# Eight weight operations ahead of the first half-step, and earlier operand loads, in a two-layer expert on one core

## The chip, the cores and the metric

The kernel runs on one core of a Trainium2 chip. The metric is the device time of one launch in microseconds. Three runs of the kernel before stand beside one profiled execution, from which all rows below come.

## The reference

Three stages follow each other. Attention (32 heads, queries averaged in pairs, 1152 keys) gives 2304 tokens of 512 values. A dense expert with an inner width of 2048 follows: this is the stage of the change. Then eight routed experts, of which each token whose skip score is above 0 takes one.

```python
def _moe_ref(x, w_in, w_out):
    h = x @ w_in                                  # 2304 x 512 by 512 x 2048
    g = h * (1.0 / (1.0 + np.exp(-1.702 * h)))
    return (g @ w_out).astype(np.float32)         # 2304 x 2048 by 2048 x 512
```

The setup multiplies the float32 weights `w_in` and `w_out` by a double-precision scalar, so both come as 64-bit floats. Only float32 accuracy is wanted at the end.

## The kernel before, in words

**Two-part operands.** TensorE multiplies in a float32 format of reduced precision (`F32R`). Each operand is therefore split into a high half and a low half, and a product takes three matmuls: high by high, high by low, low by high.

**Weights of the dense expert.** There are 16 blocks (`fb`) of 128 inner columns. A block has two units: unit 2fb is its 128 columns of `w_in` (gives `wih` and `wil`), unit 2fb+1 its 128 rows of `w_out` (`woh` and `wol`). `wload` (L423) fetches a unit of 512 KB through SP's queue into one of three `wr` buffers; `wsplit` (L432) takes the 64-bit floats apart with integer operations. A unit has seven VectorE operations on 128 x 512 elements, `v[0]` to `v[6]` (L453 to L459), and three ScalarE operations: the absolute value of the upper words (L461, needed by `v[1]`), a scaled conversion (L462, after `v[2]`, needed by `v[6]`) and the high half itself (L463, after `v[4]`). `v[6]` writes the low half. Units 0 to 3 are split during attention, units 4 to 31 (blocks 2 to 15) in the first pass of `ffn`: 28 x 7 = 196 VectorE operations.

**Order of the split.** The generator `blocks()` in `ffn` hands these operations out one at a time. `v[5]` and `v[6]` of a unit are put among the first operations of the next unit: unit u+1 yields `v[0]`, then `v[5]` of unit u, `v[1]`, `v[2]`, `v[3]`, then `v[6]` of unit u, then its own `v[4]`. `make(u)` runs between `v[3]` and `v[4]` of unit u-1; it issues the load of unit u+2 and the absolute value of unit u. The other two ScalarE operations are appended to the list `after`, and run when `act()` is called next (or earlier, where `need()` finds that the following operation depends on one). `fill(k)` takes k entries, first from the queue `fq` (routing work, empty in the first pass), then from `blocks()`.

**Passes and half-steps.** Tokens go through in six passes of `CH` = 768, 384, 256, 256, 256, 384 tokens. A pass is cut into pieces of at most 384 tokens, so the first has two, the others one. For each block and piece the loop at the end of `ffn` runs one half-step g: `layer1` of this half-step, then `layer2` of the half-step two before (`LAG`), then `rstep` and the entries of the agenda `ag` that are due. `layer1` makes 12 matmuls into one of two PSUM buffers `h` (L599), the sigmoid on ScalarE (L604), the multiplication on VectorE (L605, the last reader of `h`), the high half `gh` on ScalarE (L606), `act()`, `fill(fa)`, the low half `gl` on VectorE (L609) and `fill(fb_)`. `layer2` makes 9 matmuls of 512 columns (L624 to L626). Each engine works through its instructions in this written order. In the first pass fa and fb_ are 3 and 3 for piece 0, 3 and 4 for piece 1.

**Operands of the next pass.** `xload` (L466) fetches `X` and the reciprocals `RD`, repeated over 64 partitions, into the single buffer `xraw` through SP's queue; `xnorm` (L474, its instruction L476) multiplies them into one of four `xa` buffers, on VectorE for the second pass; `xsplit` makes `xh` (L485, ScalarE) and `xl` (L489, VectorE). For the second pass there are four of each (j = 0 to 3). The operand tiles of piece 0 of the first pass are the ones that `xsplit` overwrites, so it is due in half-step 30, after layer 1 of that half-step has read them. In half-step numbers `first[0, 12]` is 24: loads are due at 23 + 2j, products at 24 + 2j. Agenda entries that are due at the same half-step run in the order in which they were put in: j, then load, product, split.

**Before the first half-step.** Attention ends with the `dn` matmuls (L326), whose result ScalarE copies into `dr` (L327) and sends off as `DEN` with two DMA issues (L331). Then `constants()` puts a few GpSimd operations and a `memset` of VectorE (L523) in line, and half-step 0 follows.

Of the kernel before, what the change touches and what calls it, by code (L numbers as in the profile page):

```python
# [39 lines left out]
def pieces(n):  # L40
    k = -(-n // 384)
    return [(i * (n // k), n // k) for i in range(k)]
# [29 lines left out]
class Kernel:  # L72
# [5 lines left out]
    def dma(self, out, in_):  # L78
        if out.dtype == F32R:
            out = out.bitcast(F32)  # L80
        if in_.dtype == F32R:
            in_ = in_.bitcast(F32)
        self.nc.sync.dma_start(out, in_)
# [407 lines left out]
    def ffn(self, ctx):  # L491
# [22 lines left out]
        def constants():  # L514
            nc.gpsimd.memset(ONE, 1.0)
            nc.gpsimd.memset(U, 1.0)
            nc.gpsimd.affine_select(out=U, in_=U, compare_op=ALU.is_ge, fill=0.0, base=-1, pattern=[[1, P]], channel_multiplier=-1)
            nc.gpsimd.iota(idi, pattern=[[P, NT]], base=0, channel_multiplier=1)
            for t, step, base in ((w8, -1, 8), (b8, NTOK, 0)):
                nc.gpsimd.iota(i8, pattern=[[step, 8]], base=base, channel_multiplier=0)  # L520
                for i in range(3):
                    nc.gpsimd.tensor_copy(t[:, i], i8)
            V.memset(mac[0], 0.0)  # L523

        fq = []
        ag = Agenda()
# [38 lines left out]
        def fill(k):  # L565
            for _ in range(k):
                f = fq.pop(0) if fq else next(splits, None)
                if f:
                    f()

        def act():
            while after:
                after.pop(0)()
# [17 lines left out]
        def layer1(c, fb, pc, fa, fb_):  # L591
            n = pieces(CH[c])[pc][1]
            h = hp.tile([P, 512], F32, name="h", tag="h")[:, :n]
            ah, al = self.W[fb, "wih"], self.W[fb, "wil"]
            k = 0
            for d in range(ND):
                xh, xl = self.xtile(c, d, pc)
                for a, x in ((ah, xh), (ah, xl), (al, xh)):
                    nc.tensor.matmul(h, a[:, d * P:d * P + P], x, start=(k == 0), stop=(k == 3 * ND - 1))  # L599
                    k += 1  # L600
            g = gp.tile([P, 384], F32, name="g", tag="g")[:, :n]
            gh = g3.tile([P, 384], F32R, name="gh", tag="gh")[:, :n]
            gl = g3.tile([P, 384], F32R, name="gl", tag="gl")[:, :n]
            nc.scalar.activation(g, h, AF.Sigmoid, scale=1.702)  # L604
            V.tensor_tensor(g, h, g, op=ALU.mult)  # L605
            nc.scalar.activation(gh, g, AF.Copy)  # L606
            act()
            fill(fa)
            V.tensor_tensor(gl, g, gh, op=ALU.subtract)  # L609
            fill(fb_)  # L610
            G[c, fb, pc] = (gh, gl)
# [3 lines left out]
        def layer2(c, fb, pc):  # L615
            o, n = pieces(CH[c])[pc]
            gh, gl = G.pop((c, fb, pc))
            bh, bl = self.W[fb, "woh"], self.W[fb, "wol"]
            for i in range(n // P):
                t = (C0[c] + o) // P + i  # L620
                if fb == 0:
                    acc[t] = ac.tile([P, DM], F32, name=f"acc{t % 6}", tag=f"acc{t % 6}")
                ts = slice(i * P, i * P + P)
                nc.tensor.matmul(acc[t], gh[:, ts], bh, start=(fb == 0), stop=False)  # L624
                nc.tensor.matmul(acc[t], gh[:, ts], bl, start=False, stop=False)  # L625
                nc.tensor.matmul(acc[t], gl[:, ts], bh, start=False, stop=(fb == NF - 1))  # L626
# [113 lines left out]
        def rstep():  # L740
            while todo and live[0] < 3:
                grp, i = todo.pop(0)
                evac(grp, i)
                live[0] += 1
                fq.extend(lambda grp=grp, i=i, e=e: logit(grp, i, e) for e in range(9))

                def fin(grp=grp, i=i):
                    live[0] -= 1
                    if i == len(grp) - 1:
                        route(grp)  # L750
                fq.append(fin)

        constants()
        steps = [(c, fb, pc) for c in range(len(CH)) for fb in range(NF) for pc in range(len(pieces(CH[c])))]
        first = {(c, fb): g for g, (c, fb, pc) in reversed(list(enumerate(steps)))}
        LAG = 2
        for g in range(len(steps) + LAG):
            ag.now = g
            if g < len(steps):
                c, fb, pc = steps[g]  # L760
                fa, fb_ = (2, 3) if CH[c] >= 384 else (1, 2)
                if g == 2:
                    self.recip(sm, B - 1, ag, 3)
                if c == 0:
                    fa, fb_ = 3, 3 + pc
                layer1(c, fb, pc, fa, fb_)
                if fb == 0 and pc == 0 and c + 1 < len(CH):
                    for j in range(ND):
                        for q in range(len(pieces(CH[c + 1]))):
                            g0 = first[0, 12] + 2 * j - 1 if c == 0 else first[c, 4] + 2 * j  # L770
                            ag.at(g0, xload, c + 1, j, q)
                            ag.at(g0 + 1, xnorm, c + 1, j, q)
                            ag.at(first[c, NF - 1] if c == 0 else g0 + 4, xsplit, c + 1, j, q)
            if g >= LAG:
                c2, f2, p2 = steps[g - LAG]
                layer2(c2, f2, p2)
                if f2 == NF - 1:
                    if c2 == 0 and p2 == 0:
                        while splits.gi_frame:
                            fill(1)  # L780
                            act()
                        rctx.close()
                        late["o"] = self.pool(ctx, "m_o", 2)
                        late["wg"] = late["o"].tile([P, 9, DM], F32, name="wg", tag="wg", bufs=1)
                        dma(late["wg"][:, 0:8], self.wgT.partition_broadcast(P))
                        dma(late["wg"][:, 8], self.w_skip.partition_broadcast(P))
                        for d in range(ND):
                            dma(wgd[:, d, 0:8], self.wgT[:, d * P:d * P + P].rearrange("e p -> p e"))
                            dma(wgd[:, d, 8:9], self.w_skip[d * P:d * P + P].rearrange("(p a) -> p a", a=1))
                    o, n = pieces(CH[c2])[p2]  # L790
                    grp = tuple((C0[c2] + o) // P + i for i in range(n // P))
                    if c2 < len(CH) - 1:
                        todo.extend((grp, i) for i in range(len(grp)))
            if g < len(steps) + LAG - 1:
                rstep()
                ag.run(g)
            if not (self.first or todo or fq or live[0]) and self.listed == NT - CH[-1] // P:

                self.first = late["o"].tile([P, 9, DM], F32, name="first", tag="wg", bufs=1)
                for m in range(4):  # L800
                    self.first_expert_load(m)
                for m in range(8):
                    ag.at(max(g + 2 + m // 2, first[len(CH) - 1, m] + LAG + 1), self.first_expert_split, m)

                ps = hp.tile([P, 8], F32, name="cn", tag="h")
                nc.tensor.matmul(ps, ONE, mac[self.listed], start=True, stop=True)
                V.tensor_scalar(self.early, ps[:, 0:1], P - 0.5, float(P), op0=ALU.is_gt, op1=ALU.mult)
                dma(self.ids_e, self.LIST[0:P])
                V.memset(self.x_e, 0.0)
                nc.gpsimd.indirect_dma_start(  # L810
                    out=self.x_e, out_offset=None, in_=self.X2[0:C0[-1]],
                    in_offset=bass.IndirectOffsetOnAxis(ap=self.ids_e[:, 0:1].bitcast(U32), axis=0),
                    bounds_check=C0[-1] - 1, oob_is_err=False,
                )
# [270 lines left out]
```

## Time and profile before

| | us |
|---|---|
| median of three runs | 1052.24 |
| lowest, highest | 1047.6, 1054.67 |
| the profiled execution | 1049.92 |
| its span, first to last instruction | 1048.1 |
| first pass of the dense expert, first matmul to the sigmoid of half-step 32 | 442.67 to 587.33 |
| TensorE busy (share of the span) | 996.8 (95%) |
| VectorE, ScalarE, GpSimd busy | 768.9, 501.9, 454.2 |
| mean granted clock of TensorE | 0.984 |

PE is TensorE's matmuls, PEld its weight loads, DVE is VectorE, ACT ScalarE, POOL GpSimd, SP the engine whose queue issues most DMAs. A timeline row gives the start, the duration, the engine, the source line, the operation, output and inputs by the program's names, and in brackets the idle time before it with what ended it. A row of the view of waits says who waited for whom, in total, how often, and the longest. The ends of matmuls are modelled, so starts are what is compared. Engines start an operation before the record of the one before has ended, so the distance of two starts is the price of an operation in a full queue.

### The profile page before, as it was taken

How to read it: one execution, taken by the hardware profiler on the slowest of the kernel's cores; microseconds unless marked ns; L12 is line 12 of the kernel's file. 1: busy time of each engine (PE TensorE's matmuls, PEld its weight loads, DVE VectorE, ACT ScalarE, POOL GpSimd, SP SyncE). 2: the span in 40 equal slices, each digit the busy share in tenths (PEclk: the TensorE clock that was granted, in tenths of full speed). 3: DMA queues.
4: the chain of work that ended last, by engine and by line, in shares of the span. 5: the costliest groups of instructions: out<-in, count | busy, mean ns of one | idle time of the engine just before them, and what ended most of it. 6: DMA issues, size and time to landing. Idle time of an engine off the chain costs nothing. (4 is left out here: it accounts for less than half of the span.)

```text
span 1048.1 us, 18986 instructions
## 1 busy us (share of the span) xinstructions
PE 996.8 (95%) x7002; PEld 787.3 (75%) x7002; DVE 768.9 (73%) x1643; ACT 501.9 (48%) x928; POOL 454.2 (43%) x306
## 2 busy tenths in 40 slices
PE   6999999999999999999997999999999997998994
PEld 4766667666766676698886888888889885876773
DVE  7767777778877778799977689787575564656824
ACT  2555555555555554655644422332333261555723
POOL 3798999999999998500000001101111003223212
PEclk9999999999999999999999999999999998998998
DMA  4232232223333322333342520212211234738501
GB/s 166 67 101 81 81 101 82 81 81 97 97 96 96 97 72 71 99 102 122 123 132 81 173 71 16 71 33 60 71 48 44 81 115 145 266 105 285 164 21 51
DMA packets 64321, 103.34 MB, mean 99 GB/s; under 512 B 18630, under 2 KB 34630, under 8 KB 64072
## 3 DMA queue, kind: packets, MB, share of 16 engines
q1 hardware_dynamic: 60068, 96.34, 28.6%
q0 software_dynamic: 3904, 5.15, 1.6%
q8 instruction: 67, 1.10, 0.4%
q14 instruction: 54, 0.44, 0.1%
q10 hardware_dynamic: 228, 0.30, 0.1%
HBM read 90.04 MB, written 17.35 MB: 102 GB/s over the span
## 5 line engine op out<-in xcount | busy, mean ns | idle before, releaser
L233 DVE TENSOR_REDUCE mx<-xs 128x1 f32<-128x384 f32 x432 | 212.7, 550 | 75.5 <-PE xs L230 70.1
L274 ACT ACTIVATE E<-ss 128x640 f32<-128x640 f32 (+1 forms) x224 | 174.0, 787 | 149.0 <-PE ss L273 120.7
L290 POOL TENSOR_TENSOR acc<-acc,E 128x640 f32<-128x640 f32 (+1 forms) x94 | 179.4, 1909 | 16.4 <-ACT E L274 12.3
L310 PE MATMUL av<-E,v 128*64 128x256 f32 (+1 forms) x1152 | 157.1, 413 | 0.0
L599 PE MATMUL h<-xh,wih 128*128 128x384 f32 (+1 forms) x448 | 141.3, 315 | 9.9 <-ACT wih L463 7.7
L599 PE MATMUL h<-xh,wil 128*128 128x384 f32 (+1 forms) x448 | 140.0, 312 | 0.6 <-DVE wil L459 0.5
L599 PE MATMUL h<-xl,wih 128*128 128x384 f32 (+1 forms) x448 | 139.9, 312 | 0.1
L476 POOL TENSOR_TENSOR xa<-xraw 128x256 f32<-128x256 f32 (+1 forms) x16 | 15.5, 970 | 261.3 <-DMA xraw<-RD 256.1
L310 PEld LDWEIGHTS av<-E,v 128*64 128x64 f32 x1152 | 75.6, 136 | 56.0 <-issue 15.0
L626 PE MATMUL acc<-woh,gl 128*128 128x512 f32 x288 | 114.8, 399 | 0.0
L624 PE MATMUL acc<-woh,gh 128*128 128x512 f32 x288 | 114.8, 399 | 0.0
L625 PE MATMUL acc<-wol,gh 128*128 128x512 f32 x288 | 114.5, 398 | 0.0
L230 PE MATMUL xs<-kh,qh 64*128 64x384 f32 x384 | 101.9, 388 | 7.9 <-ACT kh L210 7.2
L273 PE MATMUL ss<-qh,kh 64*128 64x320 f32 (+1 forms) x576 | 107.3, 339 | 2.0 <-ACT E L274 2.0
L604 ACT ACTIVATE g<-h 128x384 f32<-128x384 f32 (+1 forms) x112 | 49.4, 441 | 116.1 <-PE h L599 116.0
L606 ACT ACTIVATE gh<-g 128x384 fp32r<-128x384 f32 (+1 forms) x112 | 53.8, 480 | 104.6 <-DVE g L605 104.6
L599 PEld LDWEIGHTS h<-xh,wih 128*128 128x128 f32 x448 | 84.2, 188 | 18.5 <-ACT wih L463 11.0
L643 DVE CUSTOM_DVE_ANT_0 junk<-xs,wg 128x512 bf16<-128x512 f32 x135 | 95.5, 707 | 2.0
L605 DVE TENSOR_TENSOR g<-h,g 128x384 f32<-128x384 f32 (+1 forms) x112 | 55.7, 497 | 55.9 <-ACT g L604 54.5
L273 PE MATMUL ss<-M,ONE 64*128 64x320 f32 (+1 forms) x576 | 94.2, 294 | 0.7 <-DMA M<-ml 0.6
L273 PE MATMUL ss<-qh,kl 64*128 64x320 f32 (+1 forms) x576 | 92.2, 293 | 0.0
L273 PE MATMUL ss<-ql,kh 64*128 64x320 f32 (+1 forms) x576 | 92.1, 293 | 0.0
(195 smaller groups left out, 2069.6 us busy)
## 6 DMA issues: line engine op xcount, KB each, us to landing
stage<-w SPq DMA_DIRECT2D x40, 512.0 KB
qd<-qT SPq DMA_DIRECT2D x16, 576.0 KB
v<-v SPq DMA_DIRECT2D x16, 576.0 KB
kr<-kT SPq DMA_DIRECT2D x15, 576.0 KB
wr<-w_in SPq DMA_DIRECT2D x16, 512.0 KB
wr<-w_out SPq DMA_DIRECT2D x16, 512.0 KB
X<-xs SPq DMA_DIRECT2D x18, 256.0 KB
out<-xs SPq DMA_DIRECT2D x18, 256.0 KB
```

Of the source, the lines that this page charges most:

```text
L230: nc.tensor.matmul(ps[:, :384], q, k[:, part * 384:part * 384 + 384], start=True, stop=True)
L233: V.reduce_max(o, ps[:, :384], axis=AX.X)
L273: nc.tensor.matmul(ps[:, u, j * w:j * w + w], k[HALF[u]], q[HALF[u], qs], start=(n == 0), stop=(n == 3))
L274: nc.scalar.activation(place(p, i), ps[:, :, :len(kbs) * w], AF.Exp, scale=0.5 / D ** 0.5)
L290: G.tensor_tensor(d["a"], d["a"], place(p, i), op=ALU.add)
L310: nc.tensor.matmul(d["av"][HALF[u], :w], d["v"][:, u, kb], e[:, u, n * w:n * w + w], start=(kb == 0), stop=(kb == KB - 1))
L599: nc.tensor.matmul(h, a[:, d * P:d * P + P], x, start=(k == 0), stop=(k == 3 * ND - 1))
L605: V.tensor_tensor(g, h, g, op=ALU.mult)
L624: nc.tensor.matmul(acc[t], gh[:, ts], bh, start=(fb == 0), stop=False)
L625: nc.tensor.matmul(acc[t], gh[:, ts], bl, start=False, stop=False)
L626: nc.tensor.matmul(acc[t], gl[:, ts], bh, start=False, stop=(fb == NF - 1))
L643: V.tensor_tensor_reduce(out=junk, in0=R[grp[i]], in1=late["wg"][:, e], op0=ALU.mult, op1=ALU.add, scale=1.0, scalar=0.0, accum_out=R[grp] ...
```

## The change

After `constants()` and before the loop over half-steps `fill(8)` is called, so the first eight VectorE operations of the 196 (with what they bring: the loads of units 6 and 7 and the absolute values of units 4 and 5) stand ahead of half-step 0; each `fill` of the pass then hands out operations eight places further on. For the second pass's operands the loads are due at 21 + 2j instead of 23 + 2j, and the products at 23 + 2j instead of 24 + 2j. The splits stay at half-step 30, and the later passes keep their places.

```diff
--- before.py
+++ after.py
@@ -751,6 +751,7 @@
                 fq.append(fin)
 
         constants()
+        fill(8)
         steps = [(c, fb, pc) for c in range(len(CH)) for fb in range(NF) for pc in range(len(pieces(CH[c])))]
         first = {(c, fb): g for g, (c, fb, pc) in reversed(list(enumerate(steps)))}
         LAG = 2
@@ -767,9 +768,9 @@
                 if fb == 0 and pc == 0 and c + 1 < len(CH):
                     for j in range(ND):
                         for q in range(len(pieces(CH[c + 1]))):
-                            g0 = first[0, 12] + 2 * j - 1 if c == 0 else first[c, 4] + 2 * j
+                            g0 = first[0, 12] + 2 * j - 3 if c == 0 else first[c, 4] + 2 * j
                             ag.at(g0, xload, c + 1, j, q)
-                            ag.at(g0 + 1, xnorm, c + 1, j, q)
+                            ag.at(g0 + 2 if c == 0 else g0 + 1, xnorm, c + 1, j, q)
                             ag.at(first[c, NF - 1] if c == 0 else g0 + 4, xsplit, c + 1, j, q)
             if g >= LAG:
                 c2, f2, p2 = steps[g - LAG]
```

## Rows read from the trace of the kernel before

**Rows 1.** Windows: us; PE, PEld, DVE, ACT, POOL busy (x); PEclk, DMA share, GB/s.

```profile
440.00:450.00 10.00, 9.67 (x61) 8.18 (x58) 5.53 (x13) 4.94 (x10) 0.00 (x0) 1.00 0.08 32
...
510.00:520.00 10.00, 10.00 (x54) 9.17 (x53) 10.00 (x24) 6.18 (x13) 0.00 (x0) 1.00 0.41 138
...
550.00:560.00 10.00, 7.04 (x28) 6.38 (x29) 8.11 (x17) 4.75 (x9) 0.00 (x0) 0.83 0.29 96
```

**Rows 2.** Waits, 440 to 590: who <- for whom: us, times, longest.

```profile
PEld h L599 <- ACT wih L463: 11.0, 7, 4.2
...
PE h L599 <- ACT wih L463: 7.7, 4, 3.7
...
DVE xa L476 <- DMA xraw<-RD: 5.2, 2, 2.8
```

**Rows 3.** Timeline, TensorE: start, us, line op out<-in xcount [idle before <-releaser].

```profile
446.93 0.34 PE L599 MATMUL h<-xh,wih 128*128 128x384 f32 x1
...
449.01 0.40 PE L624 MATMUL acc<-woh,gh 128*128 128x512 f32 x1
...
453.20 0.40 PE L624 MATMUL acc<-woh,gh 128*128 128x512 f32 x1
...
552.96 0.45 PE L599 MATMUL h<-xh,wih 128*128 128x384 f32 x1 [3.72 <-ACT wih L463]
...
566.05 0.44 PE L599 MATMUL h<-xh,wih 128*128 128x384 f32 x1 [2.90 <-ACT wih L463]
```

**Rows 4.** Timeline, ScalarE (ACTq: its DMA issues).

```profile
442.79 0.65 ACT L327 ACTIVATE dr<-dn 128x576 f32<-128x576 f32 x1 [0.99 <-PE dn L326]
...
443.47 0.55 ACTq L331 DMA_DIRECT2D DEN<-dr  x2
...
446.60 1.21 ACT L461 ACTIVATE t<-wr 128x512 f32<-128x512 f32 x2
...
516.32 0.49 ACT L604 ACTIVATE g<-h 128x384 f32<-128x384 f32 x1 [0.36 <-PE h L599]
...
551.34 0.52 ACT L606 ACTIVATE gh<-g 128x384 fp32r<-128x384 f32 x1 [3.69 <-DVE g L605]
...
552.29 0.61 ACT L463 ACTIVATE wih<-t 128x512 fp32r<-128x512 f32 x1
...
587.33 0.49 ACT L604 ACTIVATE g<-h 128x384 f32<-128x384 f32 x1 [0.96 <-PE h L599]
```

**Rows 5.** Timeline, VectorE, first pass.

```profile
441.93 0.06 DVE L523 MEMSET mac<- 128x4 uint32 x1
...
445.57 0.56 DVE L605 TENSOR_TENSOR g<-h,g 128x384 f32<-128x384 f32 x1 [3.58 <-ACT g L604]
...
450.90 0.42 DVE L454 TENSOR_SCALAR t<-t 128x512 f32<-128x512 f32 x1
...
451.23 0.68 DVE L455 SCALAR_TENSOR_TENSOR t<-wr,t 128x512 uint32<-128x512 uint32 x1
...
451.83 0.55 DVE L609 TENSOR_TENSOR gl<-g,gh 128x384 fp32r<-128x384 f32 x1
...
550.28 0.56 DVE L476 TENSOR_TENSOR xa<-xraw 128x384 f32<-128x384 f32 x1 [2.34 <-DMA xraw<-RD]
...
563.38 0.56 DVE L476 TENSOR_TENSOR xa<-xraw 128x384 f32<-128x384 f32 x1 [2.82 <-DMA xraw<-RD]
```

**Rows 6.** Timeline, VectorE, late in attention.

```profile
427.99 1.92 DVE L457 SCALAR_TENSOR_TENSOR t<-wr,t 128x512 uint32<-128x512 uint32 x1
```

**Rows 7.** Timeline, SP's DMA issues (L83).

```profile
541.49 1.56 SPq L83 DMA_DIRECT2D xraw<-X  x1
...
554.25 0.38 SPq L83 DMA_DIRECT2D wr<-w_in  x1
...
554.72 0.46 SPq L83 DMA_DIRECT2D xraw<-X  x1
```

**Rows 8.** Waits of TensorE, 590 to 857.

```profile
PE h L599 <- DVE g L605: 1.3, 1, 1.3
```

## The prediction

> **What bounds the kernel now.** I number the half-steps of the first pass g = 0 to 31 (block g // 2, piece g % 2); 32 opens the second pass. I read the windows first: at 510 to 520 us TensorE and VectorE are both busy all the time, at 550 to 560 TensorE only for 7.04 of 10 us, at a mean granted clock of 0.83 [rows 1]. The view of waits says for what: high halves of `wih` (L463 of ScalarE), 7.7 us on the matmuls and 11.0 on the weight loads before them; beside it VectorE waits 5.2 us in two places for the copy of `RD` into `xraw` [rows 2]. Then the timeline, engine by engine. Unhindered, layer 1 of a half-step takes 2.08 us (446.93 to 449.01) and a whole half-step 4.19 (449.01 to 453.20) [rows 3]. Half-step 18's sigmoid starts at 516.32, the first since half-step 0 that waits for TensorE; half-step 32's starts at 587.33 [rows 4]. That is 71.01 us for 14 half-steps that need 14 x 4.19 = 58.66. So the pass loses 12.35 us after half-step 18, and this is the most that the change can give back.
>
> Two causes, which add up. First the order: a block has 14 VectorE weight operations and two half-steps carry only 6 + 7 = 13. Counting in program order, the fifth operation of block fb's `w_in` unit (L457, after which ScalarE may write `wih`) is number 14fb - 23. For block 10 it is 117, the last of half-step 17, so `act()` converts in 18. For block 11 it is 131, the first of half-step 20, and the conversion goes into 21, directly before layer 1 of 22: from there TensorE has only one layer 2 (2.1 us) between layer 1 of 2fb-1 and layer 1 of 2fb, while sigmoid 0.49, multiplication 0.56 and the stretch from `gh` to the end of `wih` (551.34 to 552.90) make 2.6 [rows 4, 5]. Second, from there on every VectorE stall goes straight to TensorE. `xa` starts at 550.28 after a wait of 2.34 for the copy; the multiplication of half-step 25 is behind it, then `gh`, then `wih` at 552.90, and at 552.96 TensorE starts after 3.72 us idle; the same at 566.05 with 2.90 [rows 3 to 5].
>
> **Part 1: eight operations ahead.** Nothing is added to the total: 196 weight operations stay, eight of them go in front. They are six tensor-scalar operations (one every 0.33 us, 450.90 to 451.23) and two scalar-tensor-tensor (0.60, 451.23 to 451.83): 3.2 us [rows 5]. VectorE is free from 441.99 to 445.57 (3.58 idle), so they would fit, but the second needs the absolute value from ScalarE. That is queued there behind `dr` (which waits for the last `dn` matmuls until 442.79) and two DMA issues, done at 444.02; it takes 0.6 (two in 1.21) and is done at 444.68 [rows 4]. The other seven (five at 0.33, two at 0.60: 2.87) run from 444.73 to 447.6, and the multiplication of half-step 0 starts there, not at 445.57: +2.0. It frees the PSUM buffer that layer 1 of half-step 2 needs; that now starts at 446.93, then at 447.6 + 0.56 = 448.2. Cost: 1.3 us on TensorE's path. Half-steps 1 and 2 go through by 0.2 to 0.4 us by the same count, and from there VectorE gains 0.3 a half-step (six or seven operations of 0.45, two tensor-tensors of 0.47: 3.86 against 4.19), as now; it has caught up near 20. Bounds: nothing, if the eight stayed in the idle stretch; above, the dearest such operation, 1.92 us while GpSimd was adding [rows 6], for all eight. I take 1.3, since GpSimd is at 0.00 from 440 to 450 [rows 1].
>
> What it buys: with eight fewer ahead of it the fifth operation is number 14fb - 31, which is at most 13(fb - 1) for every fb up to 18. So all blocks get their conversion in half-step 2fb-2 at the latest, a half-step sooner than now, with 4.19 + 2.1 = 6.3 us for a chain of 2.6: 3.7 us of slack. The low halves follow six operations behind: the closest, block 15, is done in half-step 28 and needed in 30. The 12.35 go.
>
> **Part 2: the loads.** Now a load is called one half-step before `xnorm` needs it. Issue to use took 8.8 us in the first (541.49 to 550.28) and 8.7 in the second (554.72 to 563.38) [rows 5, 7], against a half-step of 4.19. The second was also held on SP: the weight load ahead of it in that queue waited for its buffer until 554.25. Afterwards loads are called in 21, 23, 25, 27 and `xnorm` in 23, 25, 27, 29. There is one `xraw` buffer, so load j+1 waits for `xnorm` j; both are called at the end of the same half-step, in this order. That leaves 2 x 4.19 - 0.56 = 7.8 us. So up to 1.0 us of VectorE wait may stay at each of three places, and nothing in the first. SP's weight loads keep their place: unit 29's is issued in 23, 31's in 25, both ahead of that half-step's `xload` and freed by operations already queued. Behind the waiting `xnorm` stand the next multiplication and its conversion, and 1.0 is inside the slack of 3.7. The four `xsplit` stay in 30, the last `xl` ends 4.3 us after layer 1 of 30 (sigmoid, multiplication, `gh` and four conversions at 0.5 each, one `xl` of 0.55), needed after 6.3. Cost 0. If the cover goes, what exceeds 3.7 is paid by TensorE.
>
> A price that only a page states: by the Trainium skill, "DMA: Bandwidth & Descriptors", section "Anatomy of one DMA", a DMA costs about 2.0 us plus its bytes over 436 GB/s, an estimate of 2.5 us for 192 KB. By it both copies would land inside one half-step and part 2 would move nothing. The same page's "Rules for kernel authors" says that an outermost dimension of size 2 keeps a copy on two engines; `RD`'s source begins with such a dimension. The measured 8.8 and 8.7 side with the second rule and I keep them.
>
> **The sum.** 1.3 - 12.35 = -11.05, say -11.0. In the second pass and after, nothing takes it back: from 590 to 857 TensorE's longest wait for another engine is 1.3 us [rows 8], and all later loads and gathers hang on work that moves along with it. The profiled execution took 1049.92 (span 1048.1 and 1.8 around it): 1038.9. The median of the runs is 1052.24, 0.2% more; -11.0 is -1.05%, which gives 1041.2.
>
> **Rivals.**
> (a) VectorE is the bound, not the order. It is at 10.00 of 10 us for long [rows 1]. Then only its own idle time counts: 3.2 us of operations done early less 2.0 of delay, and the 5.2 of waits: 6.4, so 1043.5 on the profile, 1045.8 on the median. Against: it does 3.86 us per 4.19, and ScalarE waits for TensorE from 516.32.
> (b) The copies land still later, because the loads of 23 and 25 now run with a weight load in front of them. At 12 us each, a third over the slowest measured, VectorE waits 4.2 at three places, 0.5 beyond the slack each, and one pause may lower the clock as between 550 and 560 (mean 0.83, so 1.7 us lost of 10) [rows 1]: gain about 8, 1044 on the median. For it: the second load had one 0.5 us ahead.
> (c) Slower: the eight operations run at the dearest price, 1.92 each [rows 6], ahead of the first multiplication. It would start at 441.99 + 15.4 = 457.4, layer 1 of half-step 2 at 457.9, 11.0 us late, and after such a pause the clock's 1.7 come on top: 12.7 against 12.35, so 1050.3 on the profile and 1052.6 on the median. It decides from about 1.9 us per operation on; each 0.1 more costs 0.8. For it: these prices were paid 14 us earlier. Against: GpSimd was adding then, and has no work from 440 to 450 [rows 1]. By the Trainium skill, "SBUF — State Buffer", section "Who interferes with whom", VectorE and GpSimd lock a shared pair of ports against each other; the 1.92 beside GpSimd's add agrees, and by that rule the eight cost 3.2 here.
> (d) It doesn't do what it says: something that I don't see in the rows (a buffer's reuse, a load) holds the same half-steps, and the time stays at 1050 to 1054.
>
> **Chances.** Forecast 0.67, (a) 0.12, (b) 0.12, (c) 0.05, (d) 0.04. About 1% (10.5 us) is what a measurement here can tell from no change. The forecast's own spread is 9 to 12.35 us of gain, 1040 to 1043.5, with 3 us on either side from run to run, so 0.7 of it lies beyond 1%: 0.47 faster. The other 0.20, (a), (b) and most of (c) and (d) lie within 1%: 0.50. Slower by more is what is left of (c) and (d): 0.03. The range holds the forecast, (a) and (b): 1036 to 1049.
>
> **What would show it.** Right: in the first pass no wait of TensorE for `wih` (now 7.7), one of about 1.3 us before layer 1 of half-step 2, the multiplication of half-step 0 at 447.6, half-step 32's sigmoid near 576.3, `xa` waits of 0 to 1 us, a granted clock of 1.00 throughout. Wrong: `wih` waits still there after 520 with VectorE full (a), `xa` waits above 3.7 (b), operations over 1 us before the first multiplication (c).

## The result, and the profile after

The kernel with the change takes 1043.32 us (median of 6 runs, 1040.43 to 1043.83), the kernel before beside it 1053.14. The ratio of the mean times is 0.9911, 95% interval 0.9885 to 0.9937, or 9.4 us less (the medians lie 9.8 apart). Measured once more beside later runs (below) it was 0.9887, 0.9864 to 0.9911, or 12 us less. The forecast was 11.0 less.

The total of one profiled execution is no good measure here. From the last sigmoid of the dense expert to the end, the same instructions took between 191.4 and 199.2 us in the twelve profiled executions of this study (eleven kernels; the change, profiled twice, took 195.3 and 195.4). So I measure the dense expert by itself, from its first matmul. To half-step 32's sigmoid the kernel before took 587.33 - 442.67 = 144.7 us, the changed one 577.09 - 443.23 = 133.9: 10.8 less, where the forecast had 11.05. To the last sigmoid it is 414.1 and 403.6.

The waits of the first pass (waiting engine and line <- what it waited for: us, times, longest), to be held against [rows 2]:

```profile
DVE xa L476 <- DMA xraw<-RD: 3.0, 2, 2.1
...
PE h L599 <- DVE g L605: 1.4, 1, 1.4
```

TensorE's 7.7 us for `wih` are gone. The one wait that its matmuls have is new, and it is the price of the eight operations. The start of the pass, on VectorE (columns as in [rows 5]):

```profile
442.47 0.42 DVE L453 TENSOR_SCALAR t<-wr 128x512 uint32<-128x512 uint32 x1
...
445.40 0.43 DVE L454 TENSOR_SCALAR t<-t 128x512 f32<-128x512 f32 x1 [2.51 <-ACT t L461]
...
448.08 0.42 DVE L454 TENSOR_SCALAR t<-t 128x512 f32<-128x512 f32 x1
448.42 0.55 DVE L605 TENSOR_TENSOR g<-h,g 128x384 f32<-128x384 f32 x1
...
546.10 0.56 DVE L476 TENSOR_TENSOR xa<-xraw 128x384 f32<-128x384 f32 x1 [2.07 <-DMA xraw<-RD]
...
554.41 0.55 DVE L476 TENSOR_TENSOR xa<-xraw 128x384 f32<-128x384 f32 x1
...
571.29 0.56 DVE L476 TENSOR_TENSOR xa<-xraw 128x384 f32<-128x384 f32 x1 [0.94 <-DMA xraw<-RD]
```

and on ScalarE and TensorE, one row each:

```profile
444.70 1.23 ACT L461 ACTIVATE t<-wr 128x512 f32<-128x512 f32 x2 [0.70 <-DMA DEN<-dr]
```

```profile
449.02 0.45 PE L599 MATMUL h<-xh,wih 128*128 128x384 f32 x1 [1.36 <-DVE g L605]
```

Of the eight, the first runs at once; the second stands for 2.51 us until ScalarE has gone through `dr` and its two DMA issues; the other seven take 445.40 to 448.42, and layer 1 of half-step 2 starts after 1.36 us of idleness. The ends of matmuls are modelled, so starts say it better: layer 1 of half-step 2 starts 449.02 - 443.23 = 5.79 us after the pass's first matmul, where it started 446.93 - 442.67 = 4.26 after it [rows 3]. That is 1.5 us later, and 1.6 with the half-step behind it. Late in the pass the windows show what [rows 1] showed as 7.04 at 0.83 (us; PE, PEld, DVE, ACT, POOL busy; clock, DMA share, GB/s):

```profile
440.00:450.00 10.00, 8.31 (x55) 6.47 (x52) 7.32 (x17) 5.54 (x11) 0.00 (x0) 1.00 0.26 93
450.00:460.00 10.00, 10.00 (x52) 9.12 (x52) 9.92 (x22) 6.53 (x14) 0.00 (x0) 1.00 0.36 111
550.00:560.00 10.00, 10.00 (x53) 9.17 (x52) 9.22 (x21) 4.68 (x10) 0.00 (x0) 1.00 0.50 149
```

### The profile page after: what moved, and what is told of

Read it like the earlier page. It is cut to its first block, busy times and chain, and to the rows that moved or that the text cites. A ratio compares the mean times of both kernels' runs of the same rounds, so it can differ in the third digit from the quotient of the medians.

```text
span 1042.1 us, 18979 instructions
## 1 busy us (share of the span) xinstructions
PE 994.9 (95%) x7002; PEld 787.0 (76%) x7002; DVE 768.2 (74%) x1643; ACT 501.3 (48%) x928; POOL 453.7 (44%) x306
```

## The experiments

My theory: the order of the weight operations and the late copies cost the pass 12.35 us together, and a half-step of slack makes it bear some wait of VectorE. Rivals: the order alone, the copies alone, or VectorE's load. In the table "pass" is from the first matmul of the dense expert to half-step 32's sigmoid and "dense" to its last sigmoid, both from the profiled execution; the ratio is that of the runs to the kernel before beside them. The rows from "eight ahead alone" to "sixteen ahead" ran on one chip, the next four on a second, the last two on a third; ratios compare best within a chip.

| kernel | pass | dense | ratio (95% interval) |
|---|---|---|---|
| before | 144.7 | 414.1 | 1 |
| the change | 133.9 | 403.6 | 0.9911 (0.9885 to 0.9937) |
| eight ahead alone | 141.7 | 413.6 | 0.9976 (0.9963 to 0.9988) |
| earlier loads alone | 138.0 | 407.9 | 0.9924 (0.9902 to 0.9945) |
| seven in each half-step, earlier loads | 135.2 | 405.6 | 0.9932 (0.9912 to 0.9952) |
| sixteen ahead, earlier loads | 140.3 | 410.8 | 0.9984 (0.9973 to 0.9996) |
| the change again | 134.4 | 403.9 | 0.9887 (0.9864 to 0.9911) |
| before, copy of `RD` in two | 138.8 | 405.4 | 0.9912 (0.9888 to 0.9935) |
| seven, earlier loads, copy in two | 132.2 | 399.4 | 0.9855 (0.9831 to 0.9879) |
| seven, loads earlier still | 133.8 | 403.8 | 0.9900 (0.9877 to 0.9923) |
| the change, copy in two | 133.8 | 400.5 | 0.9852 (0.9817 to 0.9886) |
| seven, old places, copy in two | 132.3 | 399.2 | 0.9878 (0.9845 to 0.9910) |

**1. One half of the change at a time.** First the eight operations alone:

```diff
         constants()
+        fill(8)
         steps = ...
```

> Edit: the eight operations ahead, the loads and products at their old places. Theory (order and slack): each product still waits for its copy, because a load of 7 to 9 us is called one half-step (3.9 us of VectorE work) before it is needed; three periods of two half-steps grow from 8.4 to about 11 us, 8 us in all, of which the half-step of slack takes 3.7: the pass loses 4 to 5 us again, so about 1048, some 5 below the kernel before; TensorE waits for wih once or twice late in the pass, none before 545 us. Rival 1 (the order alone made the loss): the waits of VectorE cost nothing, 1043 as with the whole change. Rival 2 (the loads alone made it): 1053 or a little more, since the start costs 1.4.

Against the kernel before the pass gained 3.0 us of the change's 10.8, and the time fell by 0.24%, 2.5 us where 5 were expected. The theory's sign holds: VectorE waits 10.6 us for copies, in three places. But the pass lost 7.9 us against the change, not 4 to 5, and not by the way expected: TensorE has no wait for `wih` at all. Layer 1 of half-step 29 waited for the multiplication that frees its PSUM buffer and stood behind a product, and layer 1 of half-step 32 for `xh` of the last product. TensorE's two late waits, and what the clock did after the first (upper row) and after the second:

```profile
563.89 0.44 PE L599 MATMUL h<-xh,wih 128*128 128x384 f32 x1 [1.79 <-DVE g L605]
...
582.97 0.69 PE L599 MATMUL h<-xh,wih 128*128 128x384 f32 x1 [2.93 <-ACT xh L485]
```

```profile
566.00:568.00 2.00, 2.00 (x7) 1.81 (x7) 2.00 (x6) 0.38 (x2) 0.00 (x0) 0.50 0.12 38
...
584.00:586.00 2.00, 2.00 (x6) 1.70 (x6) 1.11 (x2) 1.23 (x3) 0.00 (x0) 0.50 0.36 51
586.00:588.00 2.00, 2.00 (x6) 1.53 (x5) 0.56 (x1) 1.39 (x3) 0.00 (x0) 0.50 0.17 17
```

The granted clock is 0.50, the lower of its two levels (1.2 GHz of 2.4), for some 4 us after the wait of 1.79 and up to 588 after the one of 2.93; this is part of the larger loss. Now the loads alone (the change without `fill(8)`):

```diff
         constants()
-        fill(8)
         steps = ...
```

> Edit: loads and products at their new places, nothing ahead of half-step 0. Theory: the order costs what it did, 0.4 to 0.5 us at every second half-step from 20 on (about 2.5), and a wait of VectorE of up to 1 us at three products goes straight to TensorE (up to 3), while the start costs nothing: 3 to 5.5 of 12.35 stay lost, so 7 to 9 below the kernel before, about 1045. Rival 1 (order alone): 1051 to 1053. Rival 2 (loads alone): 1042, a little below the whole change, by the 1.4 that the start doesn't pay.

The pass gained 6.7 and the time fell by 0.76%, 8 us, inside the expected 7 to 9. No product waits for its copy any more, and TensorE's wait for `wih` shrinks from 7.7 us to 2.6:

```profile
PE h L599 <- ACT wih L463: 2.6, 4, 0.8
...
PE h L599 <- DVE wil L459: 0.5, 1, 0.5
```

These idle times, read against modelled ends, understate what the order alone costs. The pass takes 138.0 us, and 132.2 and 132.3 in two runs below in which TensorE never waits: 5.7 us, where the theory had 2.5. That the time came out in the expected range is therefore luck in part: the order cost more than expected, and the waits at the products, up to 3 us in the theory, didn't come.

So both single rivals fall. The halves give 3.0 and 6.7 us of the pass, 9.7 in sum, and 10.8 together; no run shows where the other 1.1 come from.

**2. The price of the start.** Sixteen operations ahead instead of eight:

```diff
-        fill(8)
+        fill(16)
```

> Edit: sixteen operations ahead instead of eight, everything else as in the change. Theory: the eight more buy nothing and run fully ahead of the first multiplication, 8 x 0.45 = 3.6 us: TensorE's pause before layer 1 of half-step 2 grows from 1.4 to about 5 us, and the time by 3.6, to about 1047 (with a lower clock after the pause up to 1.7 more). Rival (VectorE is the bound and work done early is won back later): the pause grows but the pass ends at the same time, 1043.

The pause grew by 3.74 us to 5.10, as worked out (eight at 0.45 are 3.6), and it is not won back: the pass is 6.4 us longer than with the change. The rest is the clock, which cost more than the 1.7 expected at most:

```profile
452.66 0.69 PE L599 MATMUL h<-xh,wih 128*128 128x384 f32 x1 [5.10 <-DVE g L605]
```

```profile
454.00:456.00 2.00, 2.00 (x7) 2.00 (x7) 2.00 (x6) 0.63 (x2) 0.00 (x0) 0.50 0.40 88
456.00:458.00 2.00, 2.00 (x7) 1.71 (x7) 1.82 (x5) 1.88 (x4) 0.00 (x0) 0.50 0.45 180
```

From 452.66 to 458 at 0.50 about 2.7 us of work are lost, and 3.7 + 2.7 is the 6.4. TensorE waits nowhere else in this pass, though VectorE stands 8.3 us for copies later on. So VectorE's total work is not the bound (rival (a) of the prediction): where it was, doing more of it early would have cost nothing at the end, and the standing would have cost its full length.

**3. The same lead without the start.** Fourteen operations for a block instead of thirteen, with the change's loads and nothing ahead:

```diff
-        fill(8)
...
-                    fa, fb_ = 3, 3 + pc
+                    fa, fb_ = 3, 4
```

> Edit: the new loads; nothing ahead of half-step 0, but seven operations in every half-step of the first pass instead of six and seven by turns, so 14 for a block that has 14. Theory: the conversions come a half-step sooner just as with eight ahead, VectorE needs 4.08 us for a half-step that TensorE takes 4.19 for, and the pause of 1.4 before layer 1 of half-step 2 is gone: 1.4 below the whole change, about 1042, half-step 32's sigmoid 132.5 us after the first matmul of the pass (133.9 with the change). Rival: the early half-steps have only 0.3 to 0.4 us of room, VectorE falls behind and TensorE waits there for the PSUM buffer: equal to the whole change or above, 1043 to 1046.

A miss: the pass took 135.2, not 132.5. The early half-steps went through without a wait of TensorE, so it was not the rival's reason either. The loss came at the very end. VectorE's row of the last product, SP's of its copy, and TensorE's:

```profile
573.59 0.56 DVE L476 TENSOR_TENSOR xa<-xraw 128x384 f32<-128x384 f32 x1 [5.74 <-DMA xraw<-RD]
```

```profile
564.64 0.32 SPq L83 DMA_DIRECT2D xraw<-X  x1
565.02 0.50 SPq L83 DMA_DIRECT2D xraw<-RD  x1
565.74 0.33 SPq L83 DMA_DIRECT2D wg<-wgT  x1
```

```profile
575.63 0.45 PE L599 MATMUL h<-xh,wih 128*128 128x384 f32 x1 [1.85 <-ACT xh L485]
```

With the weight operations done sooner, their buffers come free sooner, and the 2 MB load of `wg`, which reuses that memory, is issued 0.7 us behind the last copy. From the issue of the pair (`X`, then `RD`) to its use it took 573.59 - 564.64 = 8.95 us, and TensorE waited 1.85 for `xh`. In the kernel with the change `wg` follows 4.4 us behind the copy of `RD` (568.92) and the pair is used after 7.1. The eight ahead alone had the same at its last product: copy of `RD` issued at 573.18, `wg` at 573.90, 9.0 us to use, a wait of 4.38; the sixteen ahead too, with 9.0 us. That the lengthening is due to `wg` is what these times suggest, and no run shows it by itself; the next runs test the copy.

**4. Why is the copy slow?** While nothing but the copy of `RD` was running, the kernel before showed a DMA share of 0.12, two of sixteen engines, at 41 GB/s:

```profile
566.50:570.00 3.50, 3.37 (x17) 2.97 (x17) 2.16 (x6) 0.61 (x3) 0.00 (x0) 1.00 0.12 41
```

So I gave each of the two source rows a DMA of its own, in the kernel before, with every call at its old place:

```diff
-        rd = self.RD[2 * j:2 * j + 2, t0:t0 + n].rearrange("u (a n) -> u a n", a=1).to_broadcast([2, 64, n])
-        self.dma(t[:, 1, :n], rd)
+        for u in range(2):
+            self.dma(t[64 * u:64 * u + 64, 1, :n], self.RD[2 * j + u:2 * j + u + 1, t0:t0 + n].to_broadcast([64, n]))
```

> Edit: the kernel before, with the copy of RD issued as two, one for each 64 partitions, everything else at its old place. While only that copy ran (566.5 to 570 of the trace before) the DMA share was 0.12, two of sixteen engines. Theory (two engines make the copy late): each half now runs on sixteen, a load lands in 4 to 5 us instead of 8.7, VectorE's wait for copies falls from 5.2 to below 1 us with no call moved, and the pass shortens as with the loads alone, by about 6 us: 1048 to 1050 where the kernel before takes 1055. Rival (the copy is late because it queues behind the 512 KB weight loads): waits of 2 to 3 us stay, time as before, within 1 us.

No product of the first pass waits, the pass is 5.9 us shorter, and the time falls by 0.88% (0.65 to 1.12), with no call moved; the whole change gave 1.13% on the same chip (below). The rival falls: the weight loads stand in the queue as before. The last pair of copies, which ran alone in both kernels, moved its last bytes 6.6 us after its issue before and 3.5 us after it now. More came than expected: the dense expert as a whole is 8.7 us shorter, 2.8 more than the pass. In the later passes GpSimd makes the products, ScalarE waits behind them for `xh`, and its sigmoids behind that. This wait from 577 to 850 us was 13.4 us in the kernel before and is now:

```profile
ACT xh L485 <- POOL xa L476: 2.8, 3, 1.1
```

TensorE's own waits there, 1.9 us for `g` and `xh` in the kernel before, are gone too.

The change, measured beside the next runs, to have them on one chip:

> The whole change once more, on the chip on which the next three run, for a comparison with them. All theories: ratio to the kernel before 0.991 as measured first (about 9 to 10 us below it); first pass 133.9 us from its first matmul to half-step 32's sigmoid.

It came out at 0.9887, 134.4 us for the pass, with a wait for `wih` of 0.24 us in one place. Then seven in each half-step with the short copy:

> Edit: the run with seven operations in each half-step, with the copy of RD in two halves. There the last product waited 5.7 us for a copy beside which the 2 MB load of wg ran, and this undid the gain at the start. Theory (late last copy): with a copy of 4 to 5 us the wait goes below 1.5, the pass is 1.4 below the whole change (132.5 us) and the time 1.4 below it. Rival (seven each overloads VectorE): still 135 us, 1 to 2 above the whole change.

132.2 us, as expected, no wait of TensorE in the whole first pass, and 0.9855: some 3 us below the change on the same chip, where 1.4 were expected. The later passes give the rest, as with the copy in two alone (267.2 us from half-step 32 to the last sigmoid, 269.5 with the change). The last product still waited, 1.88 us instead of 5.74 (below 1.5 was expected), its copy in use 5.1 us after issue with `wg` again right behind. And the other way to bring that copy in time, calling everything two half-steps sooner:

```diff
-                            g0 = first[0, 12] + 2 * j - 3 if c == 0 else first[c, 4] + 2 * j
+                            g0 = first[0, 12] + 2 * j - 5 if c == 0 else first[c, 4] + 2 * j
```

> Edit: the run with seven operations in each half-step, loads at half-steps 19 to 25 and products at 21 to 27, a further two half-steps earlier; RD's copy as it was. Theory (late last copy, lengthened by the load of wg): the last product is done in half-step 27, before wg is asked for, its wait stays at 1 us, no wait of TensorE from half-step 2 to 32: 132.5 us for the pass and 1.4 below the whole change. Rival (seven each overloads VectorE, or a product anywhere costs the same): 134 to 135.5 us, no better than the whole change.

Half a miss: the last product no longer waits (0.7 at most anywhere), but the pass took 133.8, and the time, 0.9900, is no better than the change's on this chip. TensorE waited 0.45 and 0.57 us for the multiplication, at 557 and 566, each time behind a product: seven operations and the product in the same half-steps are about as much as VectorE can do (by an estimate from the prices above: 7 x 0.45 + 2 x 0.47 and half a product, 0.24, are 4.33 for 4.19). Here the rival has a point.

**5. What is left of each part with a short copy.** The change with the copy in two:

> Edit: the whole change with the copy of RD in two halves. Theory: the pause of 1.4 before layer 1 of half-step 2 stays, the waits for copies go, and in the later passes TensorE's waits for xh and g go as they did in the run with seven operations and two halves: first pass 133.4 to 133.8 us, last sigmoid of the dense expert 400.8 to 401.2 us after the pass's first matmul, 1.4 behind that run and some 2.7 ahead of the change. Rival (it was the seven operations, not the short copy, that brought the later passes' gain): last sigmoid at 403 or more.

133.8, as expected, and 400.5, a little better than expected: in the first pass no wait for any copy, and the 1.4 us at the start TensorE's only wait. Its ratio is 0.9852. And seven in each half-step with the loads and products at their old places:

> Edit: seven operations in each half-step and the copy of RD in two halves, loads and products at their old places. Theory (part 2 of the change only worked around the slow copy): with a short copy the earlier calls bring nothing; first pass 132.2 to 133 us, last sigmoid near 399.4, the same time as with the earlier calls within 1 us. Rival (one half-step is too short for any copy): VectorE waits of 1 us and more come back at each product and the pass takes 134 us or more.

132.3 and 399.2, the same as with the earlier calls (132.2 and 399.4); the ratio is 0.9878 on another chip, and its interval holds the 0.9855 of that run. One product waits, 0.67 us:

```profile
550.82 0.56 DVE L476 TENSOR_TENSOR xa<-xraw 128x384 f32<-128x384 f32 x1 [0.67 <-DMA xraw<-RD]
```

Its copy was issued at 545.89 with a weight load just ahead of it, and was in use after 4.9 us instead of 8.8. So part 2 of the change brings its 6.7 us only because the copy is slow. The two best kernels are 0.9852 and 0.9855 by the runs, which don't tell them apart; by the dense expert alone, seven in each half-step is 1.1 to 1.3 us ahead, near the start's price.

## Why the prediction was right, point by point

**What bounded the kernel.** Right: the loss of 12.35 us behind half-step 18 was the whole that could be had, 10.8 came back, and with the 1.6 that the start costs this is all of it. The two causes are both shown (3.0 and 6.7 us alone, 10.8 together). A step of the count was wrong, without effect on the sum: "For block 10 it is 117, the last of half-step 17, so `act()` converts in 18." `blocks()` appends a conversion only when the operation after it is asked for, here in half-step 18 behind its `act()`. So it ran in 19, directly before layer 1 of 20, which waited; the losses begin with block 10 and not with 11. ScalarE and TensorE in the kernel before:

```profile
522.35 0.61 ACT L463 ACTIVATE wih<-t 128x512 fp32r<-128x512 f32 x1
```

```profile
523.01 0.44 PE L599 MATMUL h<-xh,wih 128*128 128x384 f32 x1 [0.43 <-ACT wih L463]
```

**Part 1.** Right, and 0.3 us low: layer 1 of half-step 2 was forecast 1.3 us later and came 1.5 later (idle time in the profile 1.36). The row [rows 4] of ScalarE's queue made the sum: by VectorE's own idle time of 3.58 us the eight would have cost nothing, and by the dearest price [rows 6] 11. The absolute value ended 0.1 us later than forecast, the seven operations took 3.0 instead of 2.87. The lead of a half-step did what was said: no wait for `wih`, or 0.24 us in the second measurement.

**Part 2.** The sum was right, a step in it was not. I put up to 1.0 us of wait at the last three products and nothing at the first; it was 2.07 at the first, none at the next two and 0.94 at the last. The step that failed is "and nothing in the first". The prediction looked at the weight loads of units 29 and 31 in SP's queue, and what it says of these holds; it left out unit 28's, which stands ahead of the first `xload`. SP's queue after the change, and the operation of VectorE that frees the buffer:

```profile
536.90 0.38 SPq L83 DMA_DIRECT2D wr<-w_in  x1
537.33 0.51 SPq L83 DMA_DIRECT2D xraw<-X  x1
```

```profile
535.68 0.56 DVE L605 TENSOR_TENSOR g<-h,g 128x384 f32<-128x384 f32 x1
536.15 0.68 DVE L457 SCALAR_TENSOR_TENSOR t<-wr,t 128x512 uint32<-128x512 uint32 x1
```

`make()` issues the weight load two operations before the one that frees its buffer (L457). For unit 28 the border of half-steps 21 and 22 lies between the two: the first `xload` stood in SP's queue behind a load that could only go out after the next half-step's multiplication (535.68). TensorE had no wait behind the 2.07, which fits the 3.7 us of slack that the prediction had worked out; that the slack held for a wait twice as long as the longest foreseen is luck. With the loads alone, without this slack and with the border elsewhere, no such wait arose.

**The page's price.** An estimate of 2.5 us for the copy came from the Trainium skill, "DMA: Bandwidth & Descriptors", section "Anatomy of one DMA". That section gives it for DMAs that GpSimd issues, which the prediction left out, and this copy goes through SP's queue; its measured 7.1 us and more, from issue to use, lie far above. The rule of "Rules for kernel authors" on the same page, that an outermost dimension of 2 keeps a DMA on at most two engines, agrees with the share of 0.12 and with what the split did. The prediction had kept the measured duration, so the sum did not depend on it; but it treated the 8.8 us as given, where the rule named a cheaper cure than the earlier calls.

**The rest.** Nothing in the later passes took the gain back (269.4 us from half-step 32 to the last sigmoid before, 269.7 after). What the copies cost there, 2.8 us, the prediction didn't see, and the change doesn't touch it. The granted clock was 1.00 in the whole first pass, as said. Rivals: (a) fell with the sixteen ahead; (b) fell, as the first copy took 8.8 us from issue to use, not 12, and only its issue was late; (d) fell with the 10.8 us; (c) fell, as each operation took 0.33 to 0.60 us; but with sixteen ahead its mechanism shows, a pause and then the low clock.

## What to carry to other kernels

Work put ahead of a critical engine's first result costs what its slowest feeder in another queue makes it cost, not what the engine's own idle time suggests: follow the queue of the engine that feeds it. Before moving a late transfer earlier, look at the DMA share while it runs alone: 0.12 said that it used two of sixteen engines, and splitting it by its outermost dimension gave most of what the rescheduling gave (0.88% and 1.13% on one chip). And work that finishes sooner frees memory sooner: the transfer which waits for that memory may then run beside the one that is urgent.

## What the runs showed of the hardware that I had not expected

A copy whose source has two rows, each repeated 64 times, moved 41 GB/s at a DMA share of 0.12; as two DMAs, one for each row, the same bytes were in use, where a product still waited for them, 4.9 and 5.1 us after issue instead of 7.1 to 9.3. The clock of TensorE did not follow the length of a pause. After 1.36 us of idleness (the change), 1.85 (seven in each half-step) and the 2.90 of the kernel before [rows 3] it stayed at 1.00; after 1.79 and 2.93 (eight ahead alone), 3.72 (the kernel before) and 5.10 (sixteen ahead) it was granted 0.50 for some 3 to 7 us. After the 2.90:

```profile
566.00:568.00 2.00, 1.82 (x9) 1.51 (x10) 2.00 (x5) 0.56 (x1) 0.00 (x0) 1.00 0.20 43
```

and after the 1.85:

```profile
576.00:578.00 2.00, 1.79 (x11) 1.72 (x11) 2.00 (x5) 1.20 (x3) 0.00 (x0) 1.00 0.35 42
```

What decides between 1.79 and 1.85, or 2.90 and 2.93, stays open. And the last stage, the routed experts, took 191.4 to 199.2 us for the same instructions from one profiled execution to another, more than half of what the change gives. Whether the execution or the kernel makes that difference isn't shown, but three runs of the kernel before alone lay 7 us apart: only several runs and the stage's own length could judge the change.
